# Rows of x in natural order, two column groups' last weight rows converted together, and a new order of what goes first

## The chip, the cores and the metric

The kernel runs on one core of one Trainium2 chip. The metric is the device time of one execution in microseconds (us). Before the change three runs took 503.88, 503.54 and 502.99 us, median 503.54 us.

The core has five engines with a queue each: TensorE (PE in the rows; its weight loads are listed apart as PEld), VectorE (DVE), ScalarE (ACT), GpSimd (POOL) and SyncE (SP), which here issues all transfers between memory and the chip.

## The reference: what is computed

There are two parts. The first is a recurrence over 768 time steps for 4 batches of 8 heads with 40 numbers each (an mLSTM):

```python
m_new = np.maximum(f_gate[:, :, t] + m, i_gate[:, :, t])
f_stab = np.exp(f_gate[:, :, t] + m - m_new)
i_stab = np.exp(i_gate[:, :, t] - m_new)
C = f_stab[:, :, None, None] * C + i_stab[:, :, None, None] * np.einsum('bhd,bhe->bhde', vt, kt)
n = f_stab[:, :, None] * n + i_stab[:, :, None] * kt
h_tilde = np.einsum('bhde,bhe->bhd', C, qt)
nq = np.einsum('bhd,bhd->bh', n, qt)[:, :, None]
denom = np.maximum(np.abs(nq), 1.0)
o = 1.0 / (1.0 + np.exp(-o_gate[:, :, t]))
y[:, :, t] = o * h_tilde / denom
```

Its result, with the heads laid side by side, is x: 3072 tokens of 320 numbers. The second part is a feed-forward network with 2048 hidden units and an ELU between its layers:

```python
h = x @ w_in
g = np.where(h > 0.0, h, alpha * (np.exp(np.minimum(h, 0.0)) - 1.0))
return (g @ w_out)
```

The weights come as float64, the other inputs and the result are float32. The host hands the weights' bytes over unchanged, as pairs of 32-bit words.

## The kernel before, in words

**Tiles.** The 3072 tokens are 24 tiles of 128 tokens, t0 to t23: six chunks of time by four batches, the batches of chunk 0 first. A tile needs the state C of its batch, left by the tile four earlier. Within a tile the recurrence is done in matrix form (function `attention`): scores of queries and keys on PE (L551), a decay mask made by scans on DVE (L591; for the first two chunks the gates are spread to all partitions by PE, L577), mask times scores on DVE (L605), outputs on PE (from the carried state L619, within the tile L627), the update of C (PE L640, DVE or POOL L651, DVE L662), the denominators (DVE L669 to L675), the output gate (three ACT passes, L566), and the tile's rows of x in the buffer xf (DVE L685, L691). PE transposes xf in three pieces of 128 columns (L705); ACT and DVE split the result into a high part xh (L708) and a low part xl (L711), which PE multiplies in its faster format.

**The 384 columns of xf.** x has 320 columns, that is 128 + 128 + 64. The third piece holds the last 64 columns twice, so that one matmul with 128 rows can take the high and the low parts of the last 64 weight rows at once. Before the change these 64 columns are the last eight numbers of each of the eight heads (DA = 32 come first), and the host permutes the rows of w_in to match. The product for xf is therefore two DVE instructions: 256 columns (L685), and 2 x 64 columns read twice (L691).

**Conversions.** The weights are converted on the chip from float64, read as pairs of 32-bit words, to float32, and split into two parts, high and low (function `conversion`). One conversion takes one or two loads by SP into a buffer "wide" (three of them), two ACT passes (L322, L327), three DVE passes over a buffer "narrow" (two of them; L331, L336, L341), one POOL addition (L346), an ACT cast to the high part (L348) and a subtraction for the low part on DVE or POOL (L355). w_in's 2048 columns are four groups g0 to g3 of 512. Each group is three conversions before the change: rows 0 to 127, rows 128 to 255, and the last 64 rows, which are loaded twice, into both halves of the partitions. w_out is eight conversions of 256 hidden rows. That makes 20 conversions, c0 to c19: for g0, c0, c1, c2; w_out c3, c4; for g1, c5, c6, c7; w_out c8, c9; and the same again for g2 and g3.

**Feed-forward.** A step takes one block of two or three tiles through 128 hidden units: eight matmuls for the first layer (L747), the ELU on ACT and DVE (L755, L758, L760), a split into parts gh and gl (ACT L763, DVE or POOL L765), and three matmuls per tile for the second layer (L774). `BLOCKS` lists tiles per block; units of steps are block 0, 1 and 2 with hidden groups 0 to 7 (8 steps each, steps 0 to 23), then the same three blocks with groups 8 to 15 (steps 24 to 47), then the other six blocks with all 16 (144 steps in all). Groups 0 to 3 use g0, 4 to 7 use g1 and so on; two hidden groups share one conversion of w_out.

**Order.** Class `Plan` collects all operations with estimated durations and orders them by a greedy plan: at every moment, among the operations whose inputs are there, whose buffer is free and whose engine is idle, the one with the lowest rank starts (then the longest tail). An operation with several possible engines takes the one that would end it first. So a low rank means priority; a higher rank still runs wherever nothing better is ready. Each engine then executes its instructions strictly in the planned order. The ranks come from three places. The names in the string FIRST (t for tiles, c for conversions) get 0, 1, 2 and so on. Every other tile n gets its rank `SPACE` and `LEAD` steps ahead of the first step of its block, and every other conversion `LEAD_C` steps ahead of the step that needs it:

```python
lead[f"t{n}"] = begin[kb] - LEAD - SPACE * (len(blocks[kb]) - 1 - slot)
lead[f"c{i}"] = need[f] - LEAD_C
...
at = max([at] + [rank[x] for x in needs + [f"c{conv_of_2[f // W2N]}"]]) + 0.001
```

The last line gives a step its rank: just behind the tiles and conversions that it needs, and behind the step before. Conversions of weights for the first layer are found through `conv_of_1`, of the second through `conv_of_2`.

Of the kernel before, what the change touches and what calls it, by code (L numbers as in the profile page):

```python
# [11 lines left out]
F32 = mybir.dt.float32  # L12
# [25 lines left out]
class Plan:  # L38
# [21 lines left out]
    def op(self, engines, fn, r=(), w=(), nbytes=0):  # L60
        port = "port" in engines
        engines = {e: x for e, x in engines.items() if e != "port"}
        o = Op(engines, fn, {k[:2] for k in (*r, *w)}, nbytes, port)
        o.rank = self.rank
        for k in r:
            if k in self.writer:
                o.before.add(self.writer[k])
            self.readers.setdefault(k, []).append(o)
        for k in w:
            if k in self.writer:  # L70
                o.before.add(self.writer[k])
# [112 lines left out]
def tile_mlstm_then_elu_ffn(  # L184
# [20 lines left out]
    E = D + 1  # L205

    BLOCKS = [2, 3, 3, 3, 3, 3, 3, 2, 2]

    SPLITS = [(0, 8), (1, 8), (2, 8)]
    W2N = 2  # L210

    SPREAD_BY_PE = 2
    TMAX = max(BLOCKS)
    WMAX = max(512, W2N * DM)

    FIRST = "t0c0c2t1c1t2t3c3t4c4c5t5c8c9c7c6t6"

    LEAD, SPACE, LEAD_C = 5, 4, 3

    R2 = 64 + D  # L220
    ROWS = [slice(64 * two, 64 * two + D) for two in range(2)]
# [13 lines left out]
    def two_in(n, pool=True):  # L235
        return {"port": 1, "DVE": 0.13 + 0.0011 * n} | ({"POOL": 0.1 + 0.0023 * n} if pool else {})
# [4 lines left out]
    def act(n):  # L241
        return {"ACT": 0.17 + 0.00088 * n}
# [30 lines left out]
    w1h, w1l = [[[w[:, t] for w in w1] for t in ts] for ts in ((0, 1, 4), (2, 3))]  # L273
    w2h, w2l = [[w[:, x] for w in w2] for x in range(2)]
    R = DM - 2 * P
    DA = 2 * P // H

    convs = []
    conv_of_1 = {}
    conv_of_2 = {}  # L280
    for f in range(NF):
        g, j = divmod(f, G)
        if j == 0:
            conv_of_1[g] = range(len(convs), len(convs) + 3)
            for t in range(3):
                if t < 2:
                    src = [(slice(0, P), w_in[g, t * P : (t + 1) * P])]
                else:
                    src = [(slice(r, r + R), w_in[g, 2 * P :]) for r in (0, R)]
                convs.append((src, w1h[t][g], w1l[t][g] if t < 2 else None, G * P, f))  # L290
        if j % W2N == 0:
            conv_of_2[f // W2N] = len(convs)
            both = [w[g][:, j : j + W2N, :].rearrange("p j n -> p (j n)") for w in (w2h, w2l)]
            convs.append(([(slice(0, P), w_out[f // W2N])], *both, W2N * DM, f))

    def conversion(i):

        src, hi_out, lo_out, n, _ = convs[i]

        def wide():  # L300
            return T("wide", i, P, 2 * WMAX, dt=I32)[:, 0 : 2 * n]

        def words():
            s = wide().rearrange("p (n two) -> p n two", two=2)
            return s[:, :, 0], s[:, :, 1]

        def narrow():
            return T("narrow", i, P, WMAX, dt=I32)[:, 0:n]

        KL, KH, KN, KO = ("wide", i, 0), ("wide", i, 1), ("narrow", i), ("conv", i)  # L310

        def load(e, s, a):
            a = a.rearrange("p j n -> p (j n)") if len(a.shape) == 3 else a
            nc.sync.dma_start(wide()[s].bitcast(I64), a)

        for j, (s, a) in enumerate(src):
            op({"SP": 0.06}, lambda e, s=s, a=a: load(e, s, a), (), (KL + (j,), KH + (j,)),
               nbytes=(s.stop - s.start) * n * 8)
# [7 lines left out]
        op({"ACT": 0.2 + 0.00092 * n},
           lambda e: nc.scalar.mul(words()[0], words()[0].bitcast(U32), 2.0**-29),  # L327
           (), both[0::2])
        one_in = {"port": 1, "DVE": 0.22 + 0.0004 * n}
        op(one_in,  # L330
           lambda e: eng[e].tensor_scalar(  # L331
               narrow().bitcast(F32), narrow().bitcast(F32), HI_MIN, HI_MAX,
               op0=ALU.max, op1=ALU.min),
           (), (KN,))
        op(one_in,
           lambda e: nc.vector.tensor_scalar(  # L336
               narrow(), narrow(), 3, 0x3FFFFFFF,
               op0=ALU.logical_shift_left, op1=ALU.bitwise_and),
           (), (KN,))
        op({"port": 1, "DVE": 0.13 + 0.0011 * n},  # L340
           lambda e: nc.vector.scalar_tensor_tensor(  # L341
               out=narrow(), in0=words()[1], scalar=-0x40000000, in1=narrow(),
               op0=ALU.bitwise_and, op1=ALU.bitwise_or),
           both[1::2], (KN,))
        op({"POOL": 0.1 + 0.0023 * n},
           lambda e: nc.gpsimd.tensor_add(narrow(), narrow(), words()[0]),  # L346
           both[0::2], (KN,))
        op(act(n), lambda e: nc.scalar.copy(hi_out, narrow().bitcast(F32)), (KN,), (KO,))  # L348

        def rest(e):  # L350
            tf, hi, lo = narrow().bitcast(F32), hi_out, lo_out
            if lo is None:
                tf, hi = tf[R:], hi[R:]
                lo = hi
            eng[e].tensor_sub(lo, tf, hi.bitcast(F32))  # L355

        op(two_in(n), rest, (KN,), (KO,))


    ident = const.tile([P, P], F32, name="ident")  # L360
# [148 lines left out]
    def attention(n):  # L509
# [31 lines left out]
        def ps(which, *shape):  # L541
            return T("ps_a", (n, which), *shape)

        def xf():
            return T("xf", n, P, 3 * P)
# [133 lines left out]
           lambda e: eng[e].tensor_mul(v3()[2], v3()[2], den().to_broadcast([P, H, D])),  # L679
           (("den", n),), (KS,))  # L680


        def result(e):
            y, so = ps("y", P, H, E), v3()[2]
            nc.vector.tensor_mul(  # L685
                xf()[:, 0 : 2 * P].rearrange("p (h d) -> p h d", d=DA), y[:, :, 0:DA], so[:, :, 0:DA]
            )
            ends = [
                a[:, :, DA:D].unsqueeze(1).to_broadcast([P, 2, H, D - DA]) for a in (y, so)
            ]  # L690
            nc.vector.tensor_mul(  # L691
                xf()[:, 2 * P :].rearrange("p (two h d) -> p two h d", two=2, h=H), *ends
            )

        op({"DVE": 0.72}, result, (KY, KS), (("xf", n),))
        kb, slot = where[n]
        KX, KTP = ("x", kb), ("ps_a", (n, "tp"))
        ts = slice(slot * L, (slot + 1) * L)
# [16 lines left out]
    def ffn(u, kb, f0, f1):  # L715
# [11 lines left out]
        for f in range(f0, f1):  # L727
# [11 lines left out]
            def first_layer(e, g=g, fs=fs, h=h):  # L739
# [15 lines left out]
            op(act(N), lambda e, h=h, ff=ff: nc.scalar.activation(ff("e"), h(), AF.Relu, scale=-1.0),  # L755
               (KHP,), (KE,))
# [12 lines left out]
            def second_layer(e, f=f, g=g, j=j, ff=ff):  # L769
# [141 lines left out]
```

## Time and profile before

| | before |
|---|---|
| median of three runs | 503.54 us |
| profiled execution, its own time | 502.17 us |
| its span (first to last instruction) | 500.4 us |
| PE busy | 461.1 us (92%) |
| weight loads on PE | 436.8 us (87%) |
| DVE busy | 371.0 us (74%) |
| ACT busy | 287.5 us (57%) |
| POOL busy | 107.3 us (21%) |
| moved by DMA | 50.56 MB, mean 101 GB/s |

A row of a group of instructions gives line, engine, operation, what it writes and reads, shapes and count; then, behind the first bar, the busy time of all in us and the mean of one in ns; behind the second, the idle time of the engine just before them and what ended most of it. In a row of the order of time the first number is the start and the second the duration, both in us from the start of the span. The chain of waits is followed back from the last instruction: its rows give start, duration, and what held the chain at that time.

### The profile page before, as it was taken

Reading aid. Unit: us, or ns where it says so; the run is one execution under the profiler, and the core shown is the slowest. Engines: PE = TensorE matmul, PEld = TensorE weight load, DVE = VectorE, ACT = ScalarE, POOL = GpSimd, SP = SyncE. Lnnn points to the kernel's source line nnn. Section 1 sums busy time; section 2 is a strip of 40 time slices with the busy share of each in tenths; the row PEclk is TensorE's granted clock in tenths of the full one; section 3 lists DMA queues with packets and bytes.
Section 4 is the critical chain, followed back from the end, with each engine's and each line's share of the span. In section 5 each row is a group of like instructions: output and inputs, shape, how many; then the busy total and the mean of one; then the engine's idle time right before and its main releaser. Section 6 shows DMA issues by size and latency. Waiting matters only on the chain.

```text
span 500.4 us, 12512 instructions
## 1 busy us (share of the span) xinstructions
PE 461.1 (92%) x5006; PEld 436.8 (87%) x5006; DVE 371.0 (74%) x782; ACT 287.5 (57%) x673; POOL 107.3 (21%) x141
## 2 busy tenths in 40 slices
PE   2675575999999999999999999999999999999997
PEld 2565464999999999999999999999989999999996
DVE  8999989798798988767795677848767474456543
ACT  3657435588877445636476445645445554645764
POOL 2534557322322342010220121111010000000000
PEclk9998765999999999999999999999999999999999
DMA  7963465234543523521541331323333030100000
GB/s 187 259 206 107 145 220 155 83 126 153 149 138 115 173 67 109 151 83 42 153 124 39 110 106 45 123 68 109 100 94 106 1 96 2 41 1 1 28 1 26
DMA packets 39321, 50.56 MB, mean 101 GB/s; under 512 B 3136, under 2 KB 31712, under 8 KB 39264
## 3 DMA queue, kind: packets, MB, share of 16 engines
q1 hardware_dynamic: 39264, 49.77, 33.3%
q8 instruction: 39, 0.64, 0.5%
q14 instruction: 18, 0.15, 0.1%
HBM read 44.37 MB, written 5.39 MB: 99 GB/s over the span
## 4 chain that ended last, share of the span: by engine, by line
PE 83%; DVE 7%; DMA 5%; ACT 1%; issue 1%; SPq 1%; POOL 0%; DVEq 0%; POOLq 0%; ACTq 0%
PE h L747 35%; PE acc L774 34%; PE ps_a L551 4%; PE ps_a L627 3%; PE ps_a L619 3%; DVE w L591 2%; DMA wide<-in_w_in 2%; DMA qk<-in_qk 2%; PE ps_a L640 1%; PE ps_a L705 1%; DMA w<-f_d 1%; DVE narrow L336 1%; DVE narrow L341 1%; DMA b_d<-gatesi 1%; DMA bb<-b_d 0%
## 5 line engine op out<-in xcount | busy, mean ns | idle before, releaser
L747 PE MATMUL h<-xh,w 128*128 128x384 f32 (+1 forms) x720 | 180.6, 324 | 0.7 <-DVE e L760 0.6
L774 PE MATMUL acc<-w,gh 128*128 128x320 f32 x768 | 175.3, 315 | 0.0
L774 PEld LDWEIGHTS acc<-w,gh 128*128 128x128 f32 x768 | 128.4, 189 | 2.3 <-ACT gh L763 0.3
L747 PEld LDWEIGHTS h<-xh,w 128*128 128x128 f32 x720 | 126.3, 188 | 3.2 <-DVE e L760 1.4
L755 ACT ACTIVATE e<-h 128x384 f32<-128x384 f32 (+1 forms) x144 | 65.5, 455 | 108.4 <-PE h L747 102.6
L760 DVE SCALAR_TENSOR_TENSOR e<-e,h 128x384 f32<-128x384 f32 (+1 forms) x144 | 72.6, 506 | 66.3 <-ACT e L758 65.7
L774 PE MATMUL acc<-w,gl 128*128 128x320 f32 x384 | 119.4, 311 | 0.0
L747 PE MATMUL h<-xl,w 128*128 128x384 f32 (+1 forms) x432 | 112.7, 320 | 0.0
L765 DVE TENSOR_TENSOR gl<-e,gh 128x384 fp32r<-128x384 f32 (+1 forms) x129 | 71.0, 553 | 32.2 <-ACT gh L763 30.6
L763 ACT CAST gh<-e 128x384 fp32r<-128x384 f32 (+1 forms) x144 | 67.8, 473 | 33.8 <-DVE e L760 33.1
L747 PEld LDWEIGHTS h<-xl,w 128*128 128x128 f32 x432 | 77.0, 189 | 0.0
L774 PEld LDWEIGHTS acc<-w,gl 128*128 128x128 f32 x384 | 72.5, 189 | 0.5 <-DVE gl L765 0.4
L758 ACT ACTIVATE e<-e 128x384 f32<-128x384 f32 (+1 forms) x144 | 70.5, 490 | 3.7
L591 DVE TENSOR_TENSOR_SCAN w<-w,ident 128x512 f32<-128x512 f32 x32 | 40.4, 1265 | 5.5 <-DMA w<-f_d 5.5
L346 POOL TENSOR_TENSOR narrow<-narrow,wide 128x512 int32<-128x512 int32 (+1 forms) x20 | 30.1, 1505 | 58.0 <-DVE narrow L341 27.0
L765 POOL TENSOR_TENSOR gl<-e,gh 128x384 fp32r<-128x384 f32 (+1 forms) x15 | 14.6, 978 | 108.4 <-ACT gh L763 108.2
L551 PE MATMUL ps_a<-qk 40*128 40x128 f32 x384 | 33.8, 317 | 1.1 <-DVE xl L711 0.5
L566 ACT ACTIVATE vko<-vko 128x320 f32<-128x320 f32 x72 | 33.4, 465 | 1.7 <-DMA vko<-in_vko 0.9
L551 PEld LDWEIGHTS ps_a<-qk 40*128 40x128 f32 x384 | 28.2, 216 | 6.4 <-issue 3.0
L605 DVE TENSOR_TENSOR w<-ps_a,w 128x512 f32<-128x512 f32 x48 | 31.3, 680 | 0.7 <-PE ps_a L551 0.5
L651 POOL TENSOR_TENSOR C<-C,dec 40x164 f32<-40x164 f32 x30 | 15.4, 512 | 68.4 <-PE ps_a L619 62.2
L577 PE MATMUL h<-fgs,sel 96*128 96x128 bf16 x64 | 8.6, 294 | 17.9 <-DVE w L591 13.3
(84 smaller groups left out, 434.2 us busy)
## 6 DMA issues: line engine op xcount, KB each, us to landing
vko<-in_vko SPq DMA_DIRECT2D x24, 480.0 KB
w<-f_d SPq DMA_DIRECT2D x32, 256.0 KB
qk<-in_qk SPq DMA_DIRECT2D x48, 160.0 KB
wide<-in_w_out SPq DMA_DIRECT2D x8, 640.0 KB
wide<-in_w_in SPq DMA_DIRECT2D x8, 512.0 KB
out<-os SPq DMA_DIRECT2D x24, 160.0 KB
bb<-b_d SPq DMA_DIRECT2D x40, 80.0 KB
wide<-in_w_in SPq DMA_DIRECT2D x8, 256.0 KB
```

The source lines that it names most:

```text
L346: lambda e: nc.gpsimd.tensor_add(narrow(), narrow(), words()[0]),
L551: nc.tensor.matmul(ps(two, P, HH, L)[:, j, :], kt[rows, j, :], qt[rows, j, :], start=True, stop=True,)
L566: lambda e, fn=fn, kw=kw: nc.scalar.activation(v3()[2], v3()[2], fn, **kw), (), (KS,))
L591: nc.vector.tensor_tensor_scan(a, f, ident4.rearrange("p h t -> p (h t)"), 0.0, op0=ALU.mult, op1=ALU.add)
L605: lambda e, half=half: nc.vector.tensor_mul(w(half), ps(half, P, HH, L), w(half)),
L747: nc.tensor.matmul(h(), a[g][:, fs], m, start=(i == 0), stop=(i == len(prods) - 1))
L755: op(act(N), lambda e, h=h, ff=ff: nc.scalar.activation(ff("e"), h(), AF.Relu, scale=-1.0), (KHP,), (KE,))
L758: lambda e, ff=ff: nc.scalar.activation(ff("e"), ff("e"), AF.Exp, scale=-1.0), (), (KE,))
L760: lambda e, h=h, ff=ff: nc.vector.scalar_tensor_tensor(out=ff("e"), in0=ff("e"), scalar=-1.0, in1=h(), op0=ALU.add, op1=ALU.max),
L763: op(act(N), lambda e, ff=ff: nc.scalar.copy(ff("gh", F32R), ff("e")), (KE,), (KG,))
L765: lambda e, ff=ff: eng[e].tensor_sub(ff("gl", F32R), ff("e"), ff("gh", F32R).bitcast(F32)),
L774: nc.tensor.matmul(acc(a), x[:, sl], bw[g][:, j, :], start=(f == f0 and i == 0), stop=(f == f1 - 1 and i == 2),)
```

## The change

1. **x in natural order.** The product for xf is now one DVE instruction over all 320 columns, with the heads in their natural order. A new operation of its own copies columns 256 to 319 to 320 to 383; the plan may put it on DVE, POOL or ACT. The host no longer permutes the rows of w_in.
2. **Joint conversion.** The last 64 rows of two neighbouring column groups are loaded into the two halves of the partitions and converted together, once for g0 and g1 and once for g2 and g3. A conversion now lists where its parts go (`to`), with one cast and one subtraction for each. For the second group of a pair the high part lies in partitions 64 to 127 and the low part in 0 to 63. There are 18 conversions, with new numbers: g0 is c0 and c1, c2 serves g0 and g1, w_out's first four are c3, c4, c7 and c8, g1 is c5 and c6, g2 is c9 and c10, c11 serves g2 and g3, g3 is c14 and c15, and w_out's last four are c12, c13, c16 and c17.
3. **Order.** FIRST, LEAD, SPACE and LEAD_C have new values, and SPLITS gets a fourth entry.

```diff
-    SPLITS = [(0, 8), (1, 8), (2, 8)]
+    SPLITS = [(0, 8), (1, 8), (2, 8), (0, 16)]
...
-    FIRST = "t0c0c2t1c1t2t3c3t4c4c5t5c8c9c7c6t6"
-
-    LEAD, SPACE, LEAD_C = 5, 4, 3
+    FIRST = "t0c0c1c4t1c2c6c5c8t2c3c7c9"
+
+    LEAD, SPACE, LEAD_C = 4, 3, 2
...
-            conv_of_1[g] = range(len(convs), len(convs) + 3)
-            for t in range(3):
-                if t < 2:
-                    src = [(slice(0, P), w_in[g, t * P : (t + 1) * P])]
-                else:
-                    src = [(slice(r, r + R), w_in[g, 2 * P :]) for r in (0, R)]
-                convs.append((src, w1h[t][g], w1l[t][g] if t < 2 else None, G * P, f))
+            for t in range(2):
+                conv_of_1[g].append(len(convs))
+                convs.append(([w_in[g, t * P : (t + 1) * P]], [(slice(0, P), w1h[t][g], w1l[t][g])], G * P, f))
+            if g % 2 == 0:
+                for x in range(2):
+                    conv_of_1[g + x].append(len(convs))
+                src = [w_in[x, 2 * P :] for x in (g, g + 1)]
+                to = [(slice(x * R, (x + 1) * R), w1h[2][g + x], None) for x in range(2)]
+                convs.append((src, to, G * P, f))
...
-        op(act(n), lambda e: nc.scalar.copy(hi_out, narrow().bitcast(F32)), (KN,), (KO,))
...
-        op(two_in(n), rest, (KN,), (KO,))
+        for x, (rows, hi, lo) in enumerate(to):
+            KO = ("conv", i, x)
+
+            def upper(e, rows=rows, hi=hi):
+                nc.scalar.copy(hi[rows], narrow().bitcast(F32)[rows])
+
+            def rest(e, rows=rows, hi=hi, lo=lo):
+                to = lo[rows] if lo is not None else hi[R - rows.start : 2 * R - rows.start]
+                eng[e].tensor_sub(to, narrow().bitcast(F32)[rows], hi[rows].bitcast(F32))
+
+            op(act(n), upper, (KN,), (KO,))
+            op(two_in(n), rest, (KN,), (KO,))
...
         def result(e):
-            y, so = ps("y", P, H, E), v3()[2]
             nc.vector.tensor_mul(
-                xf()[:, 0 : 2 * P].rearrange("p (h d) -> p h d", d=DA), y[:, :, 0:DA], so[:, :, 0:DA]
+                xf()[:, 0 : H * D].rearrange("p (h d) -> p h d", d=D), ps("y", P, H, E)[:, :, 0:D], v3()[2]
             )
-            ends = [
-                a[:, :, DA:D].unsqueeze(1).to_broadcast([P, 2, H, D - DA]) for a in (y, so)
-            ]
-            nc.vector.tensor_mul(
-                xf()[:, 2 * P :].rearrange("p (two h d) -> p two h d", two=2, h=H), *ends
-            )
 
-        op({"DVE": 0.72}, result, (KY, KS), (("xf", n),))
+
+        op({"DVE": 0.49}, result, (KY, KS), (("xf", n),))
+
+        op({"port": 1, "DVE": 0.12, "POOL": 0.25, "ACT": 0.24},
+           lambda e: copy(e, xf()[:, H * D :], xf()[:, 2 * P : H * D]), (), (("xf", n),))
```

More of the change, by code (lines that the diff above doesn't have):

```diff
@@ L275, in tile_mlstm_then_elu_ffn @@
     R = DM - 2 * P
-    DA = 2 * P // H
     convs = []
-    conv_of_1 = {}
+    conv_of_1 = {g: [] for g in range(NF // G)}
     conv_of_2 = {}
@@ L293, in tile_mlstm_then_elu_ffn @@
             both = [w[g][:, j : j + W2N, :].rearrange("p j n -> p (j n)") for w in (w2h, w2l)]
-            convs.append(([(slice(0, P), w_out[f // W2N])], *both, W2N * DM, f))
+            convs.append(([w_out[f // W2N]], [(slice(0, P), *both)], W2N * DM, f))
     def conversion(i):
-        src, hi_out, lo_out, n, _ = convs[i]
+        src, to, n, _ = convs[i]
         def wide():
@@ L308, in narrow @@
             return T("narrow", i, P, WMAX, dt=I32)[:, 0:n]
-        KL, KH, KN, KO = ("wide", i, 0), ("wide", i, 1), ("narrow", i), ("conv", i)
-        def load(e, s, a):
+        KL, KH, KN = ("wide", i, 0), ("wide", i, 1), ("narrow", i)
+        at = 0
+        for j, a in enumerate(src):
             a = a.rearrange("p j n -> p (j n)") if len(a.shape) == 3 else a
[L314 to L318, printed above, removed]
+            s = slice(at, at + a.shape[0])
+            at = s.stop
+            op({"SP": 0.06},
+               lambda e, s=s, a=a: nc.sync.dma_start(wide()[s].bitcast(I64), a),
+               (), (KL + (j,), KH + (j,)), nbytes=a.shape[0] * n * 8)
         both = [(k + (j,)) for j in range(len(src)) for k in (KL, KH)]
@@ L347, in conversion @@
            both[0::2], (KN,))
-        op(act(n), lambda e: nc.scalar.copy(hi_out, narrow().bitcast(F32)), (KN,), (KO,))
[L350 to L355, printed above, removed]
-        op(two_in(n), rest, (KN,), (KO,))
+        for x, (rows, hi, lo) in enumerate(to):
[7 more added lines that the diff above has]
+            op(two_in(n), rest, (KN,), (KO,))
     ident = const.tile([P, P], F32, name="ident")
@@ L752, in ffn @@
             op({"PE": 8 * (0.006 + 0.00044 * N)}, first_layer,
-               KX + tuple(("conv", i) for i in conv_of_1[g]), (KHP, ("turn", 1)))
+               KX + tuple(("conv", i, g % 2 if len(convs[i][1]) > 1 else 0) for i in conv_of_1[g]), (KHP, ("turn", 1)))
             op(act(N), lambda e, h=h, ff=ff: nc.scalar.activation(ff("e"), h(), AF.Relu, scale=-1.0),
@@ L779, in ffn @@
             op({"PE": 3 * nt * 0.147}, second_layer,
-               (KG, KL, ("conv", conv_of_2[f // W2N])), tuple(("acc", (u, a)) for a in range(nt)) + (("turn", 2),))
+               (KG, KL, ("conv", conv_of_2[f // W2N], 0)), tuple(("acc", (u, a)) for a in range(nt)) + (("turn", 2),))
         for a, n in enumerate(tl):
@@ L879 @@
     t = np.transpose
-    heads = moe_w_in.reshape(8, 40, 2048)
     arrays = {
@@ L887 @@
         "f_gate": np.ascontiguousarray(f_gate),
-        "w_in": np.ascontiguousarray(
-            t(
-                np.concatenate([heads[:, :32].reshape(256, 2048), heads[:, 32:].reshape(64, 2048)])
-                .view(np.int64).reshape(320, 4, 512),
-                (1, 0, 2),
-            )
-        ),
+        "w_in": np.ascontiguousarray(t(moe_w_in.view(np.int64).reshape(320, 4, 512), (1, 0, 2))),
         "w_out": np.ascontiguousarray(
```

## The prediction

> **What bounds the kernel now.** I read the page's slices first, then the stretches, then VectorE (DVE) and TensorE (PE) in order of time up to 160 us.
>
> ```profile
> span 500.4 us, 12512 instructions
> PE   2675575999999999999999999999999999999997
> ```
>
> The row gives PE's busy share in 40 slices of 12.5 us, in tenths: full from the eighth slice on, not before. The stretches give the sizes, and the engine that is full instead (us; then busy time of PE, its weight loads, DVE, ACT, POOL; granted clock; DMA):
>
> ```profile
> 0.00:87.60 87.60, 52.42 (x860) 44.34 (x860) 79.50 (x166) 46.91 (x107) 42.38 (x58) 0.83 0.63 183
> 87.60:160.00 72.40, 72.40 (x586) 70.86 (x579) 62.56 (x129) 56.70 (x128) 20.43 (x19) 0.99 0.43 131
> 88.00:440.00 352.00, 351.32 (x3571) 337.09 (x3571) 261.53 (x542) 206.93 (x481) 64.15 (x82) 1.00 0.32 96
> ```
>
> Up to 87.6 us DVE is busy 79.50 of 87.60 (91%); PE idles 35.2 us and runs at a mean clock of 0.83. From 88 to 440 PE idles 0.68 us. PE's total work is fixed, so the time is decided by where DVE lets PE take over (87.6 us now), by how much PE work is behind it then, and by whether PE ever starves afterwards.
>
> ```profile
> 43.21 0.52 PE L747 MATMUL h<-xh,w 128*128 128x256 f32 x3
> 87.64 0.58 PE L747 MATMUL h<-xh,w 128*128 128x256 f32 x1
> 57.01 2.33 DVE L591 TENSOR_TENSOR_SCAN w<-h,ident 128x512 f32<-128x512 f32 x2
> 84.24 2.32 DVE L591 TENSOR_TENSOR_SCAN w<-h,ident 128x512 f32<-128x512 f32 x2
> 78.64 0.69 DVE L341 SCALAR_TENSOR_TENSOR narrow<-wide,narrow 128x512 int32<-128x512 int32 x1
> 159.28 0.49 ACT L755 ACTIVATE e<-h 128x384 f32<-128x384 f32 x1 [0.44 <-PE h L747]
> ```
>
> Only feed-forward steps 0 to 3 run before the take-over: step 3's first layer ends at 43.7, step 4's starts at 87.64. In between DVE does ten conversions in all (78.64 is the tenth) and the scans of the sixth tile (57.01) to the eighth (84.24). Steps 4 to 31 then run without a gap; 159.28 is step 32.
>
> **Order.** Ranks follow from the code. Before, the 17 names in FIRST are ranks 0 to 16: step 0 follows t3 and c3 (7), step 4 follows c7 and c6 (15), so six tiles and ten conversions go ahead of step 4. After, step 0 ranks behind c3 (10); t3 (lead 8-4-3 = 1) and t4 (lead 4) come in at 10.00x; step 4 ranks behind c7 (11); t5, t6, t7 (leads 6, 9, 12) rank among steps 6 to 12. So five tiles and nine conversions go ahead of step 4: three tiles that DVE has touched by 87.6 move behind it. The added (0, 16) changes nothing, as unit 3 was already block 0 with groups 8 to 16.
>
> What a tile costs DVE, per instruction:
>
> ```profile
> L591 DVE TENSOR_TENSOR_SCAN w<-h,ident 128x512 f32<-128x512 f32 x16 | 18.8, 1203 | 0.4 <-PE h L577 0.3
> L605 DVE TENSOR_TENSOR w<-ps_a,w 128x512 f32<-128x512 f32 x48 | 31.3, 680 | 0.7 <-PE ps_a L551 0.5
> L570 DVE TENSOR_TENSOR bb<-bb,qk 104x512 f32<-104x512 f32 x14 | 10.4, 752 | 0.1
> L651 DVE TENSOR_TENSOR C<-C,dec 40x164 f32<-40x164 f32 x2 | 1.0, 520 | 0.0
> L662 DVE TENSOR_TENSOR C<-C,ps_a 40x164 f32<-40x164 f32 x32 | 10.2, 319 | 1.6 <-PE ps_a L640 1.2
> L685 DVE TENSOR_TENSOR xf<-ps_a,vko 128x256 f32<-128x256 f32 x24 | 10.1, 422 | 0.7
> L691 DVE TENSOR_TENSOR xf<-ps_a,vko 128x128 f32<-128x128 f32 x24 | 6.7, 281 | 0.0
> L711 DVE TENSOR_TENSOR xl<-ps_a,xh 128x384 fp32r<-128x384 f32 x24 | 13.2, 551 | 0.2
> L675 DVE RECIPROCAL den<-den 128x8 f32<-128x8 f32 x24 | 4.9, 203 | 0.8
> ```
>
> The sixth tile is done in full: 2x1.203 + 2x0.680 + 0.752 + 2x0.520 + 2x0.319 + 0.703 (both xf) + 0.551 + about 0.5 for three small ones like L675 = 7.9. The seventh has scans, both L605 and L570: 4.5. The eighth has its scans: 2.4. Moved: 14.8 us of DVE.
>
> **Joint conversion.** Twelve w_in conversions become ten:
>
> ```profile
> L331 DVE TENSOR_SCALAR narrow<-narrow 128x512 f32<-128x512 f32 x12 | 5.0, 414 | 0.0
> L336 DVE TENSOR_SCALAR narrow<-narrow 128x512 int32<-128x512 int32 x12 | 5.9, 493 | 0.1
> L341 DVE SCALAR_TENSOR_TENSOR narrow<-wide,narrow 128x512 int32<-128x512 int32 x12 | 8.3, 688 | 0.2
> L346 POOL TENSOR_TENSOR narrow<-narrow,wide 128x512 int32<-128x512 int32 x12 | 16.8, 1401 | 29.7 <-DVE narrow L341 20.3 <-ACT wide L327 4.2 <-issue 3.1
> L355 DVE TENSOR_TENSOR w<-narrow,w 64x512 fp32r<-64x512 f32 x4 | 3.1, 786 | 0.1
> ```
>
> Each one removed saves DVE 0.414 + 0.493 + 0.688 = 1.60, POOL 1.40, and ACT its two passes. Casts and subtractions keep their number (two per joint conversion, now on 64 rows; L355 shows 0.786 on 64 rows, so no gain there). Four 256 KB loads go. One saving lies ahead of step 4, one much later under PE.
>
> POOL and DVE disturb each other:
>
> ```profile
> 143.83 1.72 POOL L346 TENSOR_TENSOR narrow<-narrow,wide 128x640 int32<-128x640 int32 x1 [6.79 <-ACT wide L327]
> 144.04 1.78 DVE L765 TENSOR_TENSOR gl<-e,gh 128x256 fp32r<-128x256 f32 x1
> 152.63 0.42 DVE L765 TENSOR_TENSOR gl<-e,gh 128x256 fp32r<-128x256 f32 x1
> ```
>
> The same subtraction took 1.78 us begun under L346 and 0.42 without. The Trainium skill (SBUF — State Buffer, "Who interferes with whom") has a DVE instruction with two SBUF inputs and a GpSimd one that reads SBUF exclude each other for a whole instruction; the trace agrees. By that rule the POOL pass removed ahead of step 4 would free up to 1.36 us more (estimate from these rows) and the sum would be that much lower, while a strip copy placed on POOL would give some of it back.
>
> **xf.** Two products (0.422 + 0.281 = 0.703) become one of 128x320 plus a copy of 64 columns. The nearest rows for the two:
>
> ```profile
> L792 DVE TENSOR_TENSOR os<-acc,os 128x320 f32<-128x320 f32 x8 | 3.6, 487 | 0.1
> L232 ACT COPY os<-acc 128x320 f32<-128x320 f32 x14 | 5.6, 421 | 1.8 <-PE acc L774 1.7
> L232 ACT COPY wl<-w 128x4 f32<-128x4 f32 x31 | 5.9, 194 | 23.2 <-DVE w L591 23.2
> ```
>
> So 0.49, and a copy between 0.19 and 0.42, about 0.24 by width. DVE saves between nothing (copy on DVE) and 0.21 a tile; ACT is busy 46.91 of 87.60, so I let it take the copies: five tiles, 1.0 us. PE's transposes start about 0.1 later a tile: nothing while PE idles, hidden under matmuls after.
>
> **The take-over.** DVE work ahead of step 4 is 79.50 - 14.8 - 1.6 - 1.0 = 62.1 us; at the same 91% that is 68.4 us, 19.2 earlier. But PE work that used to fit in idle time moves behind it too. Warm prices, from the chain of waits:
>
> ```profile
> 148.94 1.09 PE ps_a L551 x16
> 91.76 0.72 PE ps_a L619 x16
> 92.48 0.74 PE ps_a L627 x64
> 90.11 0.44 PE ps_a L640 x16
> 262.45 2.82 PE h L747 x16
> 267.99 2.64 PE acc L774 x18
> ```
>
> With two spreads (L577, about 0.4 each) and the transposes (about 0.5), the sixth tile is 4.3, the seventh (to L627) 3.3, the eighth (L551, L577) 1.9: 9.5 us. Net gain 19.2 - 9.5 = 9.7.
>
> **What is given back.** (a) From 68.4, steps 4 to 31 and the three tiles must keep PE fed. A step of three tiles is 2.82/2 + 2.64/2 = 2.73 on PE, of two 1.8. If nothing starves, step 32 comes 9.7 earlier, near 149.6. DVE must do 79.50 + 62.56 less about 5.5 begun for later tiles (two scans, one L605, gates: an estimate) and 5 saved by then (2x1.6 and eight tiles' 0.2) = 131.6, so 69.5 in those 81 us: 86%, the share at which the second stretch above kept PE full. But conversions now lead by 2 steps, not 3, and share DVE with t5 to t7. Bounds: 0, and the full stall of the slower rival below, 17. Nearest is the second stretch, so near the low end: 2.5. (b) SP issues loads in order:
>
> ```profile
> SPq L314 <- POOL narrow L346: 40.4, 11, 9.6
> 95.94 0.69 DVE L341 SCALAR_TENSOR_TENSOR narrow<-wide,narrow 128x512 int32<-128x512 int32 x1
> 147.21 0.82 DVE L341 SCALAR_TENSOR_TENSOR narrow<-wide,narrow 128x640 int32<-128x640 int32 x1
> ```
>
> A weight load waits for one of three "wide" buffers (longest 9.6 us), and tile loads queued behind it wait too; c4, c6, c5 and c8 now stand ahead of t1's and t2's loads. Between 0 and 9.6; other conversions fill DVE meanwhile, so 1.0. (c) Tiles t8 on lead by less (4 and 3 for 5 and 4). DVE is idle 90 of 352 us there and lower ranks fill in: between 0 and one step, 2.73, for each of six blocks; 0.5.
>
> **Sum.** -9.7 + 2.5 + 1.0 + 0.5 = -5.7 us. The profiled execution took 502.17 (span 500.4 and 1.8 around it), so 496.5 by its measure; the median of the runs, 503.54, stands 1.4 above it: **497.8 us**.
>
> **Rivals.**
> *Full gain.* Steps 4 to 7 get g1 (c2, c5, c6) before t2, so their first layers can be done before take-over, and nothing starves: 503.5 - 9.7 - about 1 = 493. For: 86% DVE share. Against: fillers only run when DVE has nothing better.
> *Gain paid back.* Deferred tiles just move the DVE limit to step 16: t5 to t7 cost 24 us of DVE beside 12 steps of about 1.0 in 42 us of PE. If POOL takes little, DVE needs 36 at 91% = 40: barely enough, so a small slip leaves 503.5. Against: POOL is busy only 20.43 of 72.40.
> *Slower: unit 3's conversions late.* Step 28 needs c9 to c16. The ten conversions from 95.94 to 147.21 came every 5.7 us. Step 16 falls near 110, step 28 near 139. If the eight only start at step 16, after the tiles, they end at 110 + 8x5.7 = 155.6: a stall of 17, net +7, 510. It loses from a pace of (29 + 9.7)/8 = 4.8 us on. For: rank 12 of c9 and the leads of 22 to 26. Against: their loads wait for nothing but a buffer, so they can fill DVE's gaps before step 16, as ten conversions were fitted in before 87.6 beside eight tiles.
> *The edit does little.* Copies on DVE, order as dense as before: only 1.6 us of DVE saved, 502.
>
> **How the numbers follow.** Forecast (gain of 4 to 8) 0.47, full gain 0.19, paid back or little 0.13, slower 0.21. A measurement of this kernel tells about 0.2%, 1 us. Faster by more 0.69 (the third case gives 0.03), the same 0.09, slower 0.22. The range takes in the full gain with room for (a) and (b) at zero, and part of the slower case: 490 to 508; the likeliest case alone has 495.5 to 499.5.
>
> **What would show it.** PE full from the sixth or seventh slice (near 68 to 72 us), only five tiles' scans before step 4's first layer, PE idle up to there near 25 us for 35; L331, L336, L341 and L346 x18 in all; xf one 128x320 product x24 near 0.49 and copies on ACT near 0.24. It is wrong if the take-over comes later than about 78 us, or if PE shows idle time on narrow or w (L346, L355) between 100 and 160 us.

## The result and the profile after

The changed kernel takes 495.3 us, the median of five runs (494.69 to 495.71); five runs of the kernel before have a median of 502.99. The ratio is 0.9849 with a 95% interval of 0.9829 to 0.9869. The profiled execution took 494.69 us where the one before took 502.17: 7.5 us less. Forecast were 497.8 us by the runs and 496.5 by the profiled measure, that is 5.7 us less.

From the page of the kernel after: span, busy times, and the slices of PE and DVE (40 slices of 12.3 us, in tenths).

```profile
span 492.6 us, 12520 instructions
PE 456.1 (93%) x5006; PEld 432.6 (88%) x5006; DVE 362.2 (74%) x752; ACT 288.4 (59%) x681; POOL 117.6 (24%) x151
PE   2535889999999999999999999999999999999997
DVE  8989898998787987965896478873678365546543
```

PE is nearly full from the fifth slice on (49 us) and full from the seventh (74 us); before it was full from the eighth (87.6 us). Its 5006 matmuls are the same ones.

The stretches of the kernel after (start and end; then length; busy time of PE, its weight loads, DVE, ACT, POOL; granted clock, DMA share, GB/s):

```profile
0.00:60.00 60.00, 29.79 (x476) 25.57 (x477) 54.28 (x113) 35.53 (x78) 24.39 (x35) 1.00 0.61 195
60.00:87.60 27.60, 25.17 (x354) 22.40 (x353) 25.00 (x54) 14.94 (x45) 16.25 (x21) 0.88 0.46 146
87.60:160.00 72.40, 72.28 (x657) 70.14 (x656) 61.14 (x127) 55.75 (x126) 22.59 (x21) 1.00 0.37 117
```

The same first two stretches of the kernel before:

```profile
0.00:60.00 60.00, 36.51 (x542) 30.88 (x542) 54.57 (x121) 33.38 (x78) 26.60 (x42) 0.94 0.64 180
60.00:87.60 27.60, 15.91 (x318) 13.46 (x318) 24.93 (x46) 13.53 (x30) 15.79 (x17) 0.58 0.62 188
```

DVE's share is the same in both (54.28 and 54.57 of 60 us, 90%). PE did 6.7 us less in the first 60 us and 9.3 more in the next 27.6. From 87.6 to 160 us it idles 0.12 us, so nothing starves there. Up to 87.6 it idles 32.65 us for 35.18 before: of the 7.8 us by which the span is shorter, only 2.5 are idle time up to there. Another 5.0 are busy time (456.1 for the page's 461.1 before) with the same matmuls. The end of a matmul is modelled, so the split is not sharp. But PE's clock was granted at 0.58 in the second stretch before and at 0.88 now, and the last section shows that matmuls take longer at the lower clock. One group of scores of queries and keys in the second stretch before:

```profile
72.68 2.08 PE L551 MATMUL ps_a<-qk 40*128 40x128 f32 x16
```

The same sixteen matmuls take 1.16 us at full clock.

Three rows of the order of time of the kernel after: the first layer of step 4, and the first ACT pass of step 8 and of step 32.

```profile
61.65 0.39 PE L746 MATMUL h<-xh,w 128*128 128x256 f32 x1
83.03 0.49 ACT L754 ACTIVATE e<-h 128x384 f32<-128x384 f32 x1 [0.64 <-PE h L746]
151.69 0.49 ACT L754 ACTIVATE e<-h 128x384 f32<-128x384 f32 x1 [0.79 <-PE h L746]
```

Step 4 starts at 61.65 (87.64 before), step 32 at 151.69 (159.28 before). From step 32 to the end of the execution it is 343.0 us now and 342.9 before. So step 32 tells the whole change, 7.6 us, and all of it is won in front of that step.

The groups of the changed lines in the kernel after (count; busy time, mean ns of one; idle time ahead):

```profile
L687 DVE TENSOR_TENSOR xf<-ps_a,vko 128x320 f32<-128x320 f32 x24 | 11.8, 491 | 0.8
L232 ACT COPY xf<-xf 128x64 f32<-128x64 f32 x16 | 3.9, 242 | 17.0 <-DVE xf L687 17.0
L343 DVE SCALAR_TENSOR_TENSOR narrow<-wide,narrow 128x512 int32<-128x512 int32 x10 | 6.9, 686 | 0.2
L358 DVE TENSOR_TENSOR w<-narrow,w 64x512 fp32r<-64x512 f32 x3 | 3.0, 1009 | 0.1
```

The parts are as forecast: one product of 0.491 us for 0.703 before, copies of 0.242 mostly on ACT, ten w_in conversions for twelve.

### The profile page after: what moved, and what is told of

Same layout as the page of the kernel before. It is cut to its first block, busy times and chain, and to the rows that moved or that the text cites. A ratio compares the mean times of both kernels' runs of the same rounds, so it can differ in the third digit from the quotient of the medians.

```text
span 492.6 us, 12520 instructions
## 1 busy us (share of the span) xinstructions
PE 456.1 (93%) x5006; PEld 432.6 (88%) x5006; DVE 362.2 (74%) x752; ACT 288.4 (59%) x681; POOL 117.6 (24%) x151
## 4 chain that ended last, share of the span: by engine, by line
PE 86%; DVE 11%; ACT 2%; issue 1%; DVEq 0%; ACTq 0%
PE h L746 36%; PE acc L773 34%; PE ps_a L555 5%; PE ps_a L631 3%; PE ps_a L623 3%; DVE w L595 2%; PE ps_a L644 1%; PE ps_a L704 1%; DVE narrow L343 1%; DVE w L358 1%; DVE narrow L333 1%; DVE e L759 1%; DVE narrow L338 1%; PE h L581 1%; DVE w L609 1%
## 5 line engine op out<-in xcount | busy, mean ns | idle before, releaser
L764 DVE TENSOR_TENSOR gl<-e,gh 128x384 fp32r<-128x384 f32 (+1 forms) x118 | 64.1, 544 | 27.0 <-ACT gh L762 23.9
L764 POOL TENSOR_TENSOR gl<-e,gh 128x384 fp32r<-128x384 f32 (+1 forms) x26 | 25.4, 978 | 63.2 <-ACT gh L762 59.0
L348 POOL TENSOR_TENSOR narrow<-narrow,wide 128x512 int32<-128x512 int32 (+1 forms) x18 | 27.4, 1523 | 41.9 <-DVE narrow L343 24.5
L555 PE MATMUL ps_a<-qk 40*128 40x128 f32 x384 | 32.4, 316 | 0.0
L563 POOL TENSOR_TENSOR va<-vko,iT 128x320 f32<-128x320 f32 x15 | 14.1, 938 | 65.6 <-issue 33.4
```

The lines of the kernel that those rows point to most:

```text
L555: nc.tensor.matmul(ps(two, P, HH, L)[:, j, :], kt[rows, j, :], qt[rows, j, :], start=True, stop=True,)
L764: lambda e, ff=ff: eng[e].tensor_sub(ff("gl", F32R), ff("e"), ff("gh", F32R).bitcast(F32)),
```

## The experiments

**How they are read.** The first group replans: the greedy plan is made anew for the edited code. The second group holds every engine's order of instructions exactly as in the kernel after, and only gives an operation other or repeated instructions. The table has the median, the ratio to the kernel before with its interval, and the first ACT pass of steps 4, 8 and 32 in the profiled execution. The kernel before had medians of 502.5, 502.7 and 502.3 us beside these runs.

| kernel | median us | ratio | step 4 | step 8 | step 32 |
|---|---|---|---|---|---|
| before | 502.99 | 1 | 89.2 | 98.5 | 159.3 |
| after | 495.3 | 0.9849 (0.9829 to 0.9869) | 62.9 | 83.0 | 151.7 |
| b_order: new order alone | 502.78 | 1.0019 (0.9993 to 1.0045) | 63.2 | 95.1 | 161.0 |
| a_oldorder: both edits, old order | 504.14 | 1.0034 (1.0021 to 1.0047) | 87.8 | 95.7 | 160.3 |
| a_sepconv: new order and xf | 501.74 | 0.9987 (0.9976 to 0.9997) | 64.7 | 92.9 | 158.9 |
| a_oldxf: new order and joint conversion | 498.99 | 0.9936 (0.9914 to 0.9957) | 64.2 | 92.3 | 158.7 |
| b_refit: before, an order fitted to it | 499.57 | 0.9934 (0.9908 to 0.9960) | 66.4 | 83.8 | 157.2 |
| b_order_dec: b_order, gates by another way | 499.10 | 0.9924 (0.9902 to 0.9947) | 65.7 | 87.8 | 155.5 |
| a_oldxf_fixed | 496.47 | 0.9874 (0.9853 to 0.9896) | 63.7 | 84.4 | 153.2 |
| a_conv_fixed | 496.26 | 0.9867 (0.9838 to 0.9896) | 64.4 | 83.2 | 151.9 |
| a_dve_early | 505.05 | 1.0049 (1.0033 to 1.0066) | 69.6 | 93.1 | 161.7 |
| a_dve_late | 497.41 | 0.9896 (0.9863 to 0.9928) | 63.4 | 81.9 | 150.5 |
| a_bd_twice | 495.18 | 0.9857 (0.9833 to 0.9882) | 62.9 | 83.4 | 152.1 |
| a_setup | 492.69 | 0.9808 (0.9779 to 0.9838) | 60.1 | 79.4 | 148.0 |

### Which part of the change brings the gain

**b_order** is the kernel before with the new order alone, its conversions numbered as they are there.

```diff
-    FIRST = "t0c0c2t1c1t2t3c3t4c4c5t5c8c9c7c6t6"
-    LEAD, SPACE, LEAD_C = 5, 4, 3
+    FIRST = "t0c0c1c4t1c2c7c6c5c9t2c3c8c10"
+    LEAD, SPACE, LEAD_C = 4, 3, 2
```

> The kernel before with the new order alone (FIRST with its names carried over to 20 conversions, the second group's last rows right behind the first's; LEAD, SPACE, LEAD_C 4, 3, 2). Theory A (the order brings most of it: three tiles of DVE work move behind step 4): 498, that is 5 below before, TensorE full from about 70 us on. Theory B (the edits bring it, since they take work off DVE, POOL and ACT, and the order only trades one delay for another): 502 to 503.

**a_oldorder** is the kernel after with the old order, **a_sepconv** the kernel after without the joint conversion, **a_oldxf** the kernel after with the old product for xf.

```diff
 a_oldorder, against after
-    FIRST = "t0c0c1c4t1c2c6c5c8t2c3c7c9"
-    LEAD, SPACE, LEAD_C = 4, 3, 2
+    FIRST = "t0c0c2t1c1t2t3c3t4c4c5t5c7c8c6t6"
+    LEAD, SPACE, LEAD_C = 5, 4, 3
 a_sepconv, against after: `convs` and `conversion` as before
-    FIRST = "t0c0c1c4t1c2c6c5c8t2c3c7c9"
+    FIRST = "t0c0c1c4t1c2c7c6c5c9t2c3c8c10"
 a_oldxf, against after: `result` and the host's rows of w_in as before
-        op({"DVE": 0.49}, result, (KY, KS), (("xf", n),))
-        op({"port": 1, "DVE": 0.12, "POOL": 0.25, "ACT": 0.24}, ...)
+        op({"DVE": 0.72}, result, (KY, KS), (("xf", n),))
```

> The kernel after the change with the old order (old FIRST with its names carried over to 18 conversions; 5, 4, 3). Theory A: the two edits save DVE 1.6 and 1.0 us ahead of step 4, at 91% busy 2.9 us of time: 500. Theory B: 496.

> After, but each column group's last 64 rows are converted on their own, loaded twice, as before (20 conversions); new order and new xf stay. Theory A: one DVE share of a conversion, 1.6 us, more ahead of step 4: 1.8 us over after, 497. Theory B: most of the gain gone, 500 or more.

> After, but with the old permuted rows of x and the two products for xf instead of one product and a strip copy. Theory A: 0.2 us of DVE a tile, five tiles ahead of step 4: 1 us over after, 496.4. Theory B: 2 to 3 over after, 498.

Measured: the order alone moves nothing that can be told (1.0019; its ten runs lie between 501.14 and 506.28), both edits with the old order make it 0.3% slower, and all together 1.5% faster. With the new order, the xf edit is worth 1.0 us without the joint conversion (502.78 to 501.74) and 3.7 with it (498.99 to 495.3); the joint conversion 3.8 without the xf edit and 6.4 with it. So the parts do not add, and both theories fell: neither the order nor the edits bring most of it alone.

Where does b_order lose? Its step 4 is as early as in the kernel after, its step 8 is 12 us later. Step 8 is the first of the block of t2, t3 and t4, and t4 is the first tile of chunk 1, which needs that chunk's gates. They are finished by an ACT pass, transposed by PE, stored to memory (b_d) and read back; only then PE can use the carried state of the tile. From the order of time of b_order: ACT's pass, PE's transpose, the store, the first matmuls from the carried state, and step 8; then PE's stretch from 80 to 90 us.

```profile
64.40 0.29 ACT L436 ACTIVATE gatesi<-gatesi 32x128 f32<-32x128 f32 x1
72.45 0.31 PE L463 MATMUL ps_a<-ident,gatesi 32*128 32x32 f32 x1
73.23 0.33 SPq L473 DMA_DIRECT2D b_d<-gatesi  x1
82.62 0.79 PE L619 MATMUL ps_a<-C,bb 104*64 104x82 f32 x16
95.08 0.49 ACT L755 ACTIVATE e<-h 128x384 f32<-128x384 f32 x1 [1.10 <-PE h L747]
...
80.00:90.00 10.00, 7.47 (x221) 6.12 (x220) 9.77 (x26) 2.38 (x9) 5.45 (x8) 1.00 0.56 162
```

The same of the kernel after, without step 8, which stands above:

```profile
61.34 0.30 ACT L440 ACTIVATE gatesi<-gatesi 32x128 f32<-32x128 f32 x1
63.23 0.22 PE L467 MATMUL ps_a<-ident,gatesi 32*128 32x32 f32 x1
63.92 0.32 SPq L477 DMA_DIRECT2D b_d<-gatesi  x1
70.36 1.36 PE L623 MATMUL ps_a<-C,bb 104*64 104x82 f32 x16
...
80.00:90.00 10.00, 9.49 (x101) 8.62 (x100) 9.60 (x22) 6.85 (x19) 3.41 (x6) 1.00 0.47 160
```

PE's transpose stands 1.6 us behind the end of ACT's pass in the kernel after, and 7.8 in b_order, where it comes later in PE's order. In a_oldxf it is 11.9:

```profile
58.91 0.29 ACT L441 ACTIVATE gatesi<-gatesi 32x128 f32<-32x128 f32 x1
71.12 0.24 PE L468 MATMUL ps_a<-ident,gatesi 32*128 32x32 f32 x1
79.81 0.79 PE L624 MATMUL ps_a<-C,bb 104*64 104x82 f32 x16
```

Step 8 follows the first matmuls from the carried state by 12.5 us in b_order and in a_oldxf and by 12.7 in the kernel after. (In a_sepconv the store leaves at 69.6, these matmuls start at 80.3 and step 8 follows 12.6 later.) In b_order and a_oldxf, step 4 begins early, PE uses up what it has, and starves before step 8. That is a reading of the rows so far; the next runs test it.

### Is it the order's fit, or the gates' way

**b_refit** is the kernel before with another string, chosen for it:

```diff
-    FIRST = "t0c0c2t1c1t2t3c3t4c4c5t5c8c9c7c6t6"
-    LEAD, SPACE, LEAD_C = 5, 4, 3
+    FIRST = "t0c0c4t1c2c1c9c7c6c5t2c3c8c10"
+    LEAD, SPACE, LEAD_C = 4, 3, 2
```

> The kernel before, without either edit, with another FIRST of the new kind (few tiles first): t0c0c4t1c2c1c9c7c6c5t2c3c8c10 and 4, 3, 2. It was picked among many strings for this code by the end that the plan gives itself. Theory P: the edits' own work is about 3 us, the rest is how well the order fits the code, so 498 to 499. Rival (the order gains nothing without the edits): 502 or more.

It gains 3.2 us over the kernel before without any edit, and 3.2 over b_order, from the order of the same names. Its step 8 comes at 83.8, as in the kernel after. But then it loses time. Its steps 8 and 16 in the order of time, and the stretch between them:

```profile
83.83 0.47 ACT L755 ACTIVATE e<-h 128x384 f32<-128x384 f32 x1
118.12 0.49 ACT L755 ACTIVATE e<-h 128x384 f32<-128x384 f32 x1 [0.21 <-PE h L747]
...
84.00:118.00 34.00, 31.97 (x468) 29.14 (x465) 30.56 (x64) 22.85 (x48) 15.25 (x18) 1.00 0.39 125
```

Eight steps take 34.3 us, of which PE idles 2.0; in the kernel after they take 28.6, of which it idles 0.6. So most of the difference of 5.7 is other PE work that falls into these steps. No run separates the waits of that stretch.

**b_order_dec** is b_order with one buffer more: the scan of the chunk's gates writes its result to a buffer of its own, and b_d is stored from that, without ACT's pass and PE's transpose on the way.

```diff
-            nc.sync.dma_start(b_d[c], i())
+            nc.sync.dma_start(b_d[c], b())
```

> The run with the new order alone (502.8), but the scan of chunk 1's gates writes a buffer of its own instead of writing over the one that TensorE must transpose first. There the transpose stood behind other work on TensorE until 72.4 us and the store of b_d left at 73.2, against 63.9 in after. Theory P with this chain: b_d leaves near 64, the first tile of chunk 1 and step 8 come about 6 to 9 us earlier, 497 to 499. Rival (DVE's sum of work sets step 8, the chain only fills the time): 502 to 503.

```profile
66.54 0.32 SPq L477 DMA_DIRECT2D b_d<-gatesb  x1
77.61 0.79 PE L623 MATMUL ps_a<-C,bb 104*64 104x82 f32 x16
87.77 0.49 ACT L759 ACTIVATE e<-h 128x384 f32<-128x384 f32 x1 [0.23 <-PE h L751]
```

The store leaves 6.7 us earlier than in b_order, step 8 begins 7.3 earlier and step 32 5.5; the median is 3.7 lower, with intervals that lie apart. The first matmuls from the carried state are 5.0 earlier (77.61 for 82.62). So the late gates held up b_order's step 8 by most of that; the other 2.3 us lie between these matmuls and step 8. The plan was made anew, so a part of the 3.7 may be due to its other order.

### What an edit is worth when the order stays

**a_oldxf_fixed** has the old two products in place of the new one, and nothing in place of the copy. **a_conv_fixed** gives the first joint conversion the engines' work back that it saves: repeats of its own instructions on ACT and DVE, and a copy on POOL (0.69 us, where the addition saved takes 1.4). The loads that are saved do not come back.

```diff
 a_oldxf_fixed
-        op({"port": 1, "DVE": 0.12, "POOL": 0.25, "ACT": 0.24},
-           lambda e: copy(e, xf()[:, H * D :], xf()[:, 2 * P : H * D]), (), (("xf", n),))
+        op({"port": 1, "DVE": 0.12, "POOL": 0.25, "ACT": 0.24}, lambda e: None, (), (("xf", n),))
 a_conv_fixed, in conversion(i)
+   AF.Abs activation on ACT:    ... for _ in range(3 if i == 2 else 1)
+   max/min tensor_scalar, DVE:  ... for _ in range(5 if i == 2 else 1)
+   after the addition, POOL:    nc.gpsimd.tensor_copy(narrow(), narrow()) if i == 2
```

> After, with the two old products for xf (and the permuted rows) put in place of the one product and the strip copy, while every other instruction stands in the same order on every engine: the plan is not made anew. Theory W (an edit is worth the DVE work that it saves): 0.2 us a tile, five tiles before step 4: 1 us over after, 496.3. Theory P (an edit is worth what the plan makes of it: without it the greedy plan lays out another order, in which the first tile of chunk 1 is late): also about 1 here, against the 3.7 of the replanned run. A rival to both, that the strip copy itself shortens a chain: 498.5 to 499 as in the replanned run.

> After, with the work of the conversion that was saved ahead of step 4 put back into c2 as repeats: ACT's first pass three times (1.34 us more), DVE's first pass five times (1.66 us more), one more POOL pass; the order of all else stays. Theories W and P: 1.7 to 1.8 us over after, 497.1. The rival (a conversion is worth the 6.4 of the replanned run): 501 to 502.

The xf edit is worth 1.2 us by the medians and 1.5 at step 32. The conversion is worth 1.0 by the medians and 0.2 at step 32, less than the 1.8 expected. Both intervals overlap that of the kernel after, and step 32 of one execution is no sharper: a_dve_late, below, executes the same instructions as the kernel after up to 178 us, and its step 32 comes 1.2 us earlier. So these sizes are rough; but both are far from the 3.7 and 6.4 that the same edits seemed to be worth when the plan was made anew.

### Does DVE's sum ahead of the take-over decide

**a_dve_early** does the subtraction for xl five times over in tiles 0 to 3, 16 more in all. **a_dve_late** does 16 more too, in tiles 8 to 23.

```diff
-            lambda e: nc.vector.tensor_sub(xs("l"), ps("tp", P, 3, L), xs("h").bitcast(F32)),
+            lambda e: [nc.vector.tensor_sub(...) for _ in range(5 if n < 4 else 1)],    # a_dve_early
+            lambda e: [nc.vector.tensor_sub(...) for _ in range(2 if n >= 8 else 1)],   # a_dve_late
```

> After, with the subtraction for xl of each of the first four tiles done five times (16 more of 0.55 us on DVE, 8.8 us), all else in the same order. Theory W (DVE's sum of work ahead of the take-over sets it): 8 to 10 us over after, 504. Rival (the waits of the chunk 1 chain leave room): 499 or less.

> After, with the same 16 subtractions added one each to tiles 8 to 23. Theory W: hidden behind TensorE, 495.3 to 496. Rival (DVE limits later stretches too): 500 or more.

From the groups and the order of time of a_dve_early:

```profile
L710 DVE TENSOR_TENSOR xl<-ps_a,xh 128x384 fp32r<-128x384 f32 x40 | 22.2, 554 | 2.0 <-ACT xh L707 1.3
69.16 2.92 DVE L710 TENSOR_TENSOR xl<-ps_a,xh 128x384 fp32r<-128x384 f32 x5
161.72 0.49 ACT L754 ACTIVATE e<-h 128x384 f32<-128x384 f32 x1 [0.79 <-PE h L746]
```

From the order of time and the stretches of a_dve_late:

```profile
150.54 0.49 ACT L754 ACTIVATE e<-h 128x384 f32<-128x384 f32 x1 [0.81 <-PE h L746]
160.00:480.00 320.00, 318.61 (x3449) 304.02 (x3448) 223.26 (x465) 175.56 (x419) 52.61 (x75) 1.00 0.26 78
```

The kernel after in the same stretch:

```profile
160.00:480.00 320.00, 319.65 (x3462) 305.98 (x3461) 217.49 (x451) 176.62 (x423) 54.39 (x75) 1.00 0.26 78
```

16 x 0.554 = 8.9 us of DVE work early move steps 8 and 32 by 10.0 and the median by 9.8. Five subtractions in a row take 2.92 us, so each repeat takes 0.59 with its gap and all 16 take 9.5: nearly all of the delay is the repeats themselves, and the 1/0.91 of DVE's share is not needed for it. The first layer of step 4 starts 6.7 later (68.31), behind the repeats of three tiles (12 x 0.59 = 7.1); those of the fourth tile come behind it and still cost their time. So what counts is DVE's work up to step 8, and step 4's start does not mark the end of DVE's limit.

The same work late lets PE idle 1.39 us for 0.35 between 160 and 480 us and costs 2.1 by the medians, with intervals that just overlap. From step 32 to the end it takes 345.1 us for 343.0, which is 2.1 too. So most of it is hidden.

### Is the gates' way the bound in the kernel after too

**a_bd_twice** stores chunk 1's gates to another place in memory first and copies them from there to b_d, which makes their way longer and nothing else.

```diff
-            nc.sync.dma_start(b_d[c], i())
+            if c == 1: nc.sync.dma_start(b_x, i()); nc.sync.dma_start(b_d[c], b_x)
+            else: nc.sync.dma_start(b_d[c], i())
```

> After, with the store of chunk 1's gates (b_d) going through a second buffer in memory: one more transfer of 16 KB in the chain, some 2 us, all else in the same order. Theory P with this chain: step 8 comes 2 us later and so does the end, 497 to 498. Rival (DVE has other work meanwhile): 495.5 to 496.

```profile
67.44 2.33 SPq L517 DMA_DIRECT2D bb<-b_d  x6
71.01 1.23 PE L631 MATMUL ps_a<-C,bb 104*64 104x82 f32 x14
152.09 0.49 ACT L762 ACTIVATE e<-h 128x384 f32<-128x384 f32 x1 [0.79 <-PE h L754]
```

The readback starts 2.1 us later than in the kernel after (67.44 for 65.33), the matmuls behind it 0.65 later and step 32 0.4; the median does not move. The clock records of the two executions agree within 0.1 us, so they can be compared. So the gates have about 1.5 us of slack there. They are the bound where the transpose stands late, not in the kernel after. The theory that they decide in every version fell.

### Less work on DVE at the start

**a_setup** is the kernel after with seven small operations at the start moved off DVE (the zeroing of one buffer of qk, one of bb and two of C to POOL, three casts for `sel` to ACT), one put on it (`first`), in an order otherwise the same.

```diff
-        nc.gpsimd.memset(first, 0.0)
+        nc.vector.memset(first, 0.0)
-                eng[e].tensor_copy(sel[rows], ident[rows, rows])
+                nc.scalar.copy(sel[rows], ident[rows, rows])
-        eng[e].memset(t[32:64], 0.0)                        # all but qk's buffer 0
+        nc.gpsimd.memset(t[32:64], 0.0)
-        eng[e].memset(C[b], 0.0)
+        nc.gpsimd.memset(C[b], 0.0)
```

> After, with one qk memset, one bb memset and both C memsets taken from DVE to POOL, the three sel casts to ACT and the memset of first to DVE: 3.3 us of DVE work less ahead of the first gate instruction at 6.2 us, all else in the same order. Theory W: the first gates are there by about 4, so everything on DVE moves up by about 2: 493 to 493.5. Rival (the gates' or first loads' landing holds the start): 495.

From the order of time of a_setup, the scan of chunk 0's gates:

```profile
2.90 0.47 DVE L428 TENSOR_TENSOR_SCAN gatesm<-gatesf,m,gatesi 32x128 f32<-32x128 f32 x1
```

The scan in the kernel after:

```profile
6.29 0.47 DVE L428 TENSOR_TENSOR_SCAN gatesm<-gatesf,m,gatesi 32x128 f32<-32x128 f32 x1
```

The scan starts 3.4 us earlier and step 32 3.7. The median is 492.69, 2.6 under the kernel after and 1.9% under the kernel before. The intervals of a_setup and of the kernel after overlap between 0.9829 and 0.9838, so that it is the faster of the two rests also on step 32.

## Why the prediction was right or wrong

**Right: what decides.** DVE's early work sets the time. a_dve_early bears it out from the one side (9.5 us with its gaps cost 9.8) and a_setup from the other (3.4 us at the start bring 2.6 to 3.7). It is the work up to step 8, though, not only that ahead of step 4. The time behind step 32 did not change (343.0 and 342.9), so term (c), smaller leads of later tiles, 0.5, measured 0.1.

**Term by term.** The net gain of the take-over was forecast at 9.7 and the give-back at 4.0. Step 32 came 7.6 earlier, so 2.1 was given back for the 2.5 of (a) and the 1.0 of (b): their sum was taken 1.4 too large, and no run separates the two. PE idles 2.4 us between 60 and 87.6 and next to nothing from there to 160. About 1 us of the 2.1 seems to go with the clock of that execution: a_dve_late, with full clock from 52.8 us on, has step 8 at 81.86 and step 32 at 150.54 with the same instructions up to there. The slower rival, unit 3's conversions late, did not happen: PE is busy 72.28 of 72.40 us where it would have starved. The tests for "wrong" (a take-over later than 78 us, idle time on narrow or w) did not come up.

**Off in place: the take-over.** It was forecast at 68.4. Step 4 began at 61.65, but PE was full only from 74 on. "Five tiles and nine conversions go ahead of step 4" took ranks for a sequence; the greedy plan let step 4 run as soon as its own inputs were there. Only four tiles' scans and eight whole conversions stand ahead of it on DVE; the fifth tile's scans and all but the first DVE pass of the ninth conversion come at 63 us and later. DVE's busy time up to 61.65 is 55.7 us for the 62.1 of the sum. Step 32 came 2.1 us later than the forecast for no starving (149.6) all the same: what began 6.7 us earlier ran less densely up to 87.6, at half clock for 6.8 us of it.

**Wrong: the shares of the parts.** The sum gave 14.8 us of DVE work to the order and 2.6 to the edits, as if they added. b_order shows no gain that can be told for the order alone, and a_oldorder 0.3% lost by the edits alone. The step that failed is "three tiles that DVE has touched by 87.6 move behind" the take-over: that they move is not enough, the first tile of chunk 1 has to be ready for step 8 in time. With the new order on the old code it is 12 us late, as its gates are transposed late; b_order_dec shows this wait. The prediction looked at the first take-over and then for conversions; it had no term for the gates. The forecast came out because the order fits this code, which the profile before could not show and the prediction did not work out. So that the size came out is in part luck. Rival four, "the edit does little", named 502 for an order as dense as before; that is where b_order landed, by another way.

**Wrong: where the gain is seen.** "PE idle up to there near 25 us for 35" fell: PE idles 30.2 of the 61.65 us up to step 4 and 32.6 up to 87.6, for 35.2, and its busy time fell 5.0. The PE work moved behind the take-over was priced warm. That was right for the seventh and eighth tile (scores of 1.16 us at 84.32 and 96.58), not for the sixth (2.08 at 68.35, at half clock). But in its old place much of that work had run at half clock (2.08 at 72.68), so the gain could not all come from idle time. The mean clock of 0.83 that the prediction reads up to 87.6 is too high: the trace has no clock record before 33.7 us, and the profile counts such time as full clock, though the scores at 10.46 took 2.08 there too.

**Small terms.** xf's product (0.49 forecast, 0.491), the copies (0.24 on ACT, 0.242) and 18 conversions are right; ACT took 16 of the 24 copies. The joint conversion's last subtractions were costed at 0.786 as before. Two of the four stood beside an addition of POOL:

```profile
34.49 2.37 DVE L358 TENSOR_TENSOR w<-narrow,w 64x512 fp32r<-64x512 f32 x2
```

```profile
34.69 1.62 POOL L348 TENSOR_TENSOR narrow<-narrow,wide 128x512 int32<-128x512 int32 x1 [1.70 <-DVE narrow L343]
```

The first of the pair began ahead of the addition and took 0.68; the second began under it and took 1.66, ending at 36.86, behind the addition's end at 36.31. The third one on DVE took 0.69. So the pair lost about 1.0 us, ahead of the take-over. The Trainium skill (SBUF — State Buffer, "Who interferes with whom") says that such a pair of instructions shut each other out, and the rows agree. The prediction had used that rule for up to 1.36 us more gain from the POOL pass removed; a_conv_fixed shows 0.2 to 1.0 for the engines' work of the whole conversion, so no such extra is seen. It puts no POOL pass back at the old place, though, so it does not test the extra by itself.

**What stays open.** Which waits cost b_refit its time between steps 8 and 16, how much of b_order_dec's 3.7 us belongs to its new plan, and why the edits under the old order made the kernel slower. No run makes the gates of the kernel after as late as those of b_order (a_bd_twice makes them 2.1 us later), so that late gates are what holds b_order back rests on b_order_dec.

## What to carry to other kernels

Where a planner orders the work, cost an edit with the order held fixed, and then fit the order anew: edits worth about 1 us each looked like 4 to 6 us, or like a loss, only because the plan fitted or not. After the first take-over look for the next step whose inputs come from another chain, and trace that chain (here gates, transpose, store, readback) as closely as the first. Work of the engine that is full at the start costs its full time, even in the first 6 us, and the same work later is mostly hidden.

## What the runs showed of the hardware

**A mean clock can cover time without a clock record.** Scores of queries and keys in the kernel after, sixteen matmuls each time, and the clock in stretches around three of them:

```profile
10.46 2.08 PE L555 MATMUL ps_a<-qk 40*128 40x128 f32 x16
60.56 1.16 PE L555 MATMUL ps_a<-qk 40*128 40x128 f32 x16
68.35 2.08 PE L555 MATMUL ps_a<-qk 40*128 40x128 f32 x16
96.58 1.16 PE L555 MATMUL ps_a<-qk 40*128 40x128 f32 x16
...
51.00:67.00 16.00, 12.58 (x169) 11.01 (x170) 14.49 (x38) 12.46 (x34) 9.01 (x12) 1.00 0.35 112
68.00:74.00 6.00, 6.00 (x104) 5.30 (x103) 5.09 (x11) 3.36 (x9) 5.44 (x6) 0.50 0.69 207
75.00:160.00 85.00, 84.36 (x847) 81.33 (x847) 72.68 (x151) 63.20 (x147) 28.15 (x29) 1.00 0.38 120
```

Where the trace has a clock record, clock and duration agree: 1.16 us at 1.00 and 2.08 at 0.50. The first clock record of this trace begins at 50.7 us, and the profile counts the time ahead of it as 1.00; the scores at 10.46 took 2.08 all the same. The first 62 us of the kernel after, then of a_dve_late, which does the same work there and has clock records from 15.3 us on:

```profile
0.00:62.00 62.00, 31.79 (x498) 27.28 (x499) 56.06 (x121) 36.88 (x82) 24.87 (x36) 1.00 0.61 197
```

```profile
0.00:62.00 62.00, 31.68 (x495) 27.54 (x495) 55.70 (x119) 36.75 (x82) 24.36 (x35) 0.72 0.61 195
```

PE's busy times are 0.1 apart, so the 1.00 and the 0.72 differ by the records and hardly by the speed. The 0.58 and 0.88 of the stretch from 60 to 87.6 us above are measured: records cover it in both kernels. For the time ahead of the first record the durations decide.

**Small first loads are there early.** In a_setup DVE could scan the gates at 2.90 us, so their loads had landed by then. The scan's start at 6.29 in the kernels before and after was due to DVE's own work ahead of it.
